# Chunk-wise loads and transposes, 256-token first blocks and an early exponential table in an attention and max-FFN kernel

## The chip, the cores and the metric

The kernel runs on one core of one Trainium2 chip. The metric is the time of one execution on the device in microseconds (us); lower is better. The kernel before took 203.25 us (median of 3 runs, 203.05 to 204.17).

Engines are named as in the profile: PE multiplies matrices, DVE and ACT do vector and scalar work, POOL does general work and issues most DMAs here, SP and ACT issue the rest. A DMA is a data transfer. "PEclk" in the profile is the granted PE clock as a share of full speed. Some executions fall in a slower state (of the changed kernel's four, two at 215.96 and 216.19 us against 211.87 and 213.48); each run is marked fast or slow, and comparisons here use fast runs alone. Spans read from a trace are about 1.8 us shorter than the run's time.

## The reference

```python
# q, k, v: (4, 8, 768, 64) = batch, head, token, dim;  n_sink = 4, window = 128
scores = q @ k.T / sqrt(64)
keep   = (key < n_sink) | (0 <= query - key < window)      # sink tokens and a sliding window
a      = softmax(where(keep, scores, -1e9))
x      = (a @ v) laid out as (3072 tokens, 512)
h      = max(x @ w1, x @ w2, x @ w3)                       # each (512, 768)
out    = h @ w_out                                         # (768, 512), float32
```

The kernel counts twelve chunks of 256 tokens, three to a batch of 768 tokens. Heads are handled in two groups of four.

## The kernel before

The kernel builds a list of tasks. Each has an engine, an assumed cost, what it depends on and a wished-for time. A planner (`arrange`) walks through assumed time and from that fixes the order of instructions on each engine. It does this while the kernel is built; on the chip the order stays. So an assumed number that is wrong changes an order, and in the traces below an instruction of DVE or POOL that waits holds up what stands behind it (DVE stands still for 13.60 us on one load).

```python
rate = 0.30                                    # assumed MB per us of one load

def load(name, mb, want, f, eng="POOL", cost=0.65, deps=()):
    t = task(eng, cost, f, deps=deps, want=want, name="i" + name)
    dma_done[name] = task("DMA", mb / rate, lambda: None, deps=[t], want=want, lat=2.0, name=name)
    return dma_done[name]

def sink_v(b, want):                           # the sink tokens' v, as a block-diagonal matrix
    def f():
        for g in range(NQ):                    # 2 groups x 4 heads x 2 = 16 copies of 0.5 KB per batch
            for i in range(4):
                for c in (1, 2):
                    j = 2 * g + c - 1
                    nc.sync.dma_start(
                        out=vbd[32 * j + 4 * i:32 * j + 4 * i + 4, b, j, 65 * i:65 * i + 65],
                        in_=vbufs[b % 2][0:n_sink, 4 * g + i, 0, :])
    ...
    t = task("SP", 1.6, f, deps=deps, want=want, name=f"vbd{b}")

# loads of batches 1 to 3: one row of 24 token rows per partition (the flat form)
nc.gpsimd.dma_start(out=raws[b, nm, g].rearrange("p j d -> p (j d)"),
                    in_=src[b, 4 * g:4 * g + 4].rearrange("i (p j) d -> (i p) (j d)", j=24))

BLOCKS = [[0], [1, 2], [3, 4], [5, 6], [7, 8], [9, 10], [11]]   # chunks of each FFN block
```

The line `vbd<-v_sb` in a profile is one of `sink_v`'s copies; `o<-vbd,e_sink` is the product that needs them (attention to the sink tokens, from chunk 1 on). `h<-xT,w_sb` are the FFN's first products, `y<-wo_sb,h_sb` its last, and `qT<-q_raw` a transpose on DVE.

The softmax here doesn't subtract the row's maximum and nothing guards it: scores larger than these inputs give would overflow.

## Time and profile before

| read from | before |
|---|---|
| median time | 203.25 us |
| span of the profiled run | 200.7 us |
| PE busy, up to 50 us (sum of five windows) | 30.8 of 50 us |
| DVE busy, 50 to 80 us | 29.3 of 30 us |
| FFN blocks begin (timeline of PE) | 18.9, 47.7, 79.2, 107.5, 135.4, 163.0, 185.6 us |

This is the first part of the page of the kernel before: its span, busy times, and then the span in 40 equal slices of 5 us, one digit a slice (busy tenths; 9 is 90% or more).

```profile
span 200.7 us, 4228 instructions
PE 172.7 (86%) x1680; PEld 95.7 (48%) x1680; DVE 135.7 (68%) x290; ACT 95.1 (47%) x146; POOL 36.7 (18%) x56
...
PE   0127997588979997999998999989999989999892
DVE  4358497587999999999917758636677276571450
...
PEclk9999999759999999999999999999999999999999
DMA  7999999999999910409920200140000410002202
```

Up to slice 10 (50 us) PE has holes while the DMA row is full: loads bind. From there DVE is full up to slice 20, and PE still has holes up to slice 16 (80 us): DVE binds. After that PE is full but for the last slices.

The next lines are from the timeline of the kernel before; columns are start in us, duration, engine, line, operation, output and inputs, shapes, count, and in brackets the idle time ahead of it and what ended it.

```profile
8.11 11.41 SPq L324 DMA_DIRECT2D vbd<-v_sb  x16
...
25.83 0.28 PE L412 MATMUL o<-vbd,e_sink 128*128 128x260 bf16 x1
26.89 0.82 POOL L237 DMA_DIRECT2D wo_sb<-in_moe_w_out_dram  x1 [0.45 <-DMA w_sb<-in_moe_w_dram]
28.33 0.56 POOL L258 DMA_DIRECT2D q_raw<-in_q_dram  x1 [0.62 <-DMA w_sb<-in_moe_w_dram]
...
42.71 3.76 PE L529 MATMUL y<-wo_sb,h_sb 128*128 128x512 bf16 x12
...
47.69 0.59 PE L510 MATMUL h<-xT,w_sb 128*128 128x512 bf16 x2
...
79.23 6.22 PE L510 MATMUL h<-xT,w_sb 128*128 128x512 bf16 x28
```

The sixteen sink copies of batch 0 occupy SP's sequencer for 11.4 us, from 8.1 us on; SP issues nothing else until 45.8 us, so they hold up no load there. POOL issues w_out's load at 26.9 us and goes straight on to chunk 3's q at 28.3 us. The attention product of chunk 1 runs at 25.8 us.

### The profile page before, as it was taken

Reading aid. Unit: us, or ns where it says so; the run is one execution under the profiler, and the core shown is the slowest. Engines: PE = TensorE matmul, PEld = TensorE weight load, DVE = VectorE, ACT = ScalarE, POOL = GpSimd, SP = SyncE. Lnnn points to the kernel's source line nnn. Section 1 sums busy time; section 2 is a strip of 40 time slices with the busy share of each in tenths; the row PEclk is TensorE's granted clock in tenths of the full one; section 3 lists DMA queues with packets and bytes.
Section 4 is the critical chain, followed back from the end, with each engine's and each line's share of the span. In section 5 each row is a group of like instructions: output and inputs, shape, how many; then the busy total and the mean of one; then the engine's idle time right before and its main releaser. Section 6 shows DMA issues by size and latency. Waiting matters only on the chain.

```text
span 200.7 us, 4228 instructions
## 1 busy us (share of the span) xinstructions
PE 172.7 (86%) x1680; PEld 95.7 (48%) x1680; DVE 135.7 (68%) x290; ACT 95.1 (47%) x146; POOL 36.7 (18%) x56
## 2 busy tenths in 40 slices
PE   0127997588979997999998999989999989999892
PEld 0023676433445544455554455554555544454770
DVE  4358497587999999999917758636677276571450
ACT  0344562634447548434668245665266592223422
POOL 7997648233200000022000000000000000000000
PEclk9999999759999999999999999999999999999999
DMA  7999999999999910409920200140000410002202
GB/s 125 207 160 154 197 172 198 213 180 172 255 173 177 195 63 1 156 4 80 82 106 1 105 4 0 42 170 0 3 0 5 157 52 3 0 0 106 108 0 104
DMA packets 41012, 19.72 MB, mean 98 GB/s; under 512 B 29472, under 2 KB 35872, under 8 KB 40992
## 3 DMA queue, kind: packets, MB, share of 16 engines
q0 software_dynamic: 36256, 12.07, 56.8%
q1 hardware_dynamic: 4352, 6.85, 9.6%
q10 hardware_dynamic: 384, 0.52, 1.0%
q8 instruction: 13, 0.21, 0.4%
q14 instruction: 7, 0.06, 0.1%
HBM read 25.17 MB, written 6.29 MB: 157 GB/s over the span
## 4 chain that ended last, share of the span: by engine, by line
PE 66%; DVE 21%; DMA 5%; issue 3%; ACT 3%; SPq 1%; DVEq 0%; ACTq 0%
PE h L510 39%; PE y L529 13%; PE st L390 6%; DMA q_f<-in_q_dram 5%; DVE kT L286 4%; DVE h_sb L521 4%; DVE x L434 4%; PE o L421 4%; DVE e_sb L403 4%; DVE qT L286 3%; PE xt L444 2%; ACT e_sb L395 2%; PE o L412 2%; DVE rc L431 1%; SPq L160 1%
## 5 line engine op out<-in xcount | busy, mean ns | idle before, releaser
L510 PE MATMUL h<-xT,w_sb 128*128 128x512 bf16 (+1 forms) x504 | 103.7, 353 | 1.8 <-ACT xT L451 1.2
L521 DVE TENSOR_TENSOR h_sb<-h,h_sb 128x512 bf16<-128x512 f32 (+1 forms) x84 | 51.4, 616 | 26.1 <-PE h L510 20.3
L510 PEld LDWEIGHTS <-w_sb 128*128 128x128 bf16 x504 | 46.8, 99 | 38.5 <-issue 2.6
L395 ACT ACTIVATE e_sb<-st 128x1024 bf16<-128x1024 f32 (+1 forms) x48 | 44.4, 953 | 14.4 <-PE st L390 14.4
L519 ACT CAST h_sb<-h 128x512 bf16<-128x512 f32 (+1 forms) x42 | 22.1, 526 | 47.6 <-PE h L510 47.3
L529 PE MATMUL y<-wo_sb,h_sb 128*128 128x512 bf16 x144 | 33.9, 387 | 0.1
L403 DVE TENSOR_TENSOR e_sb<-e_sb,mask 128x1024 bf16<-128x1024 bf16 (+1 forms) x48 | 29.7, 640 | 5.1 <-ACT e_sb L395 4.9
L390 PE MATMUL st<-qT,kT 32*128 32x128 bf16 (+1 forms) x512 | 15.9, 253 | 16.5 <-DVE kT L286 9.3
L536 ACT COPY y_sb<-y 128x512 f32<-128x512 f32 x24 | 14.1, 586 | 21.5 <-PE y L529 17.6
L390 PEld LDWEIGHTS <-kT 32*128 32x128 bf16 x512 | 10.9, 98 | 25.0 <-DVE kT L286 9.9
L434 DVE TENSOR_TENSOR x<-o,rc 128x256 bf16<-128x256 f32 x48 | 20.4, 424 | 1.7
L431 DVE RECIPROCAL rc<-o 128x4 f32<-128x4 f32 x48 | 8.5, 177 | 19.2 <-PE o L421 19.2
L529 PEld LDWEIGHTS <-h_sb 128*128 128x128 bf16 x144 | 13.8, 99 | 15.5 <-issue 1.6
L421 PEld LDWEIGHTS <-e_sb 128*128 128x128 bf16 x352 | 17.4, 102 | 6.5 <-DVE e_sb L403 1.5
L421 PE MATMUL o<-v_sb,e_sb 128*128 128x65 bf16 x352 | 19.4, 201 | 1.1 <-DVE h_sb L521 0.6
L451 ACT COPY xT<-xt 128x512 bf16<-128x512 bf16 x24 | 14.1, 588 | 9.2 <-PE xt L444 9.1
L444 PE MATMUL xt<-ident,x 128*128 128x128 bf16 x96 | 12.3, 230 | 5.1 <-DVE x L434 4.2
L265 POOL DMA_DIRECT2D v_sb<-in_v_dram x6 | 8.5, 1429 | 41.8 <-PE o L421 40.2
L286 DVE STREAM_TRANSPOSE kT<-k_raw 128x256 f32<-128x256 f32 x18 | 13.8, 826 | 0.0
L286 DVE STREAM_TRANSPOSE qT<-q_raw 128x256 f32<-128x256 f32 x18 | 13.7, 820 | 0.0
L444 PEld LDWEIGHTS <-x 128*128 128x128 bf16 x96 | 7.2, 99 | 12.5 <-DVE x L434 8.1
L412 PE MATMUL o<-vbd,e_sink 128*128 128x260 bf16 x32 | 9.2, 287 | 0.0
(35 smaller groups left out, 51.5 us busy)
## 6 DMA issues: line engine op xcount, KB each, us to landing
out_dram<-y_sb SPq DMA_DIRECT2D x24, 256.0 KB
w_sb<-in_moe_w_dram POOLq DMA_DIRECT2D x9, 256.0 KB, 8.4
q_raw<-in_q_dram POOLq DMA_DIRECT2D x6, 384.0 KB, 16.9
k_raw<-in_k_dram POOLq DMA_DIRECT2D x6, 384.0 KB, 16.6
v_sb<-in_v_dram POOLq DMA_DIRECT2D x6, 384.0 KB, 16.0
vbd<-v_sb SPq DMA_DIRECT2D x64, 0.5 KB
v_sb<-in_v_dram POOLq DMA_DIRECT2D x6, 128.0 KB, 7.7
wo_sb<-in_moe_w_out_dram POOLq DMA_DIRECT2D x1, 768.0 KB, 9.8
```

Source lines behind the costliest of these rows:

```text
L286: nc.vector.transpose(dst, src)
L390: nc.tensor.matmul(ps[:, i, col:col + n], lhsT=kT[r, key0:key0 + 128, e], rhs=qT[r, qq:qq + n, e], start=(e == 0), stop=(e == 1))
L395: nc.scalar.activation(st["e"][:, 2 * hh:2 * hh + 2, lo:], st["ps"][:, 2 * hh:2 * hh + 2, lo:], AF.Exp, scale=scale)
L403: nc.vector.tensor_tensor(out=ee, in0=ee, in1=m.unsqueeze(1).to_broadcast([128, 2, ncol]), op=ALU.mult)
L421: nc.tensor.matmul(o[:, i, :], lhsT=st["e"][:, i, col:col + 128], rhs=vbufs[b % 2][:, 4 * g + i, kb, :], start=(c == 0 and n == 0), stop=( ...
L434: nc.vector.tensor_tensor(out=st["x"][:, tt], in0=o[:, :, :D], in1=rc.unsqueeze(2).to_broadcast([128, 4, D]), op=ALU.mult)
L444: nc.tensor.transpose(st["xt"][:, n, 128 * tt:128 * tt + 128], x[:, 128 * n:128 * n + 128], ident)
L451: nc.scalar.copy(xTs[blk][:, 2 * g:2 * g + 2, off:off + 256], st["xt"])
L510: nc.tensor.matmul(ps[:, :ntok], lhsT=w_sb[:, wi, d, fb * 128:fb * 128 + 128], rhs=xTs[blk][:, d, :ntok], start=(d == 0), stop=(d == DSUB ...
L519: nc.scalar.copy(hs, ps[:, :ntok])
L521: nc.vector.tensor_tensor(out=hs, in0=ps[:, :ntok], in1=hs, op=ALU.max)
L529: nc.tensor.matmul(ps, lhsT=box["h"][:, fb, 128 * m:128 * m + 128], rhs=wo_sb[:, fb, :], start=(fb == 0), stop=(fb == FSUB - 1))
```

## The change

Its intent: load and transpose q and k of every batch by chunks of 256 tokens instead of by whole batches, so that a chunk can start earlier and transposes are cheaper; let the first FFN blocks have one chunk each; load less through SP and ACT at the start and load ACT's exponential table meanwhile. Beside this it moves the sink copies from SP to POOL, adds a product on POOL and two transposes on DVE that nothing uses, and raises the planner's `rate`. The core of the diff, cut, with some comments added:

```diff
-    rate = 0.30
+    rate = 0.40
...
-    for g in range(NQ):
-        load(f"q0{g}0", 0.26, g - 2000, qk_first("q", q, g), eng="SP", cost=0.4)
-        load(f"k0{g}0", 0.26, g - 2000, qk_first("k", k, g), eng="ACT", cost=0.4)
+    load("q0.0", 0.26, -2000, qk_first("q", q, 0), eng="SP", cost=2.7)
+    load("k0.0", 0.26, -2000, qk_first("k", k, 0), eng="ACT", cost=2.7)
...
+    task("ACT", 1.5, warm, deps=[t_one], want=-1999, name="warm")        # exponential table
+    def probe_pool():                                    # its result is used by nothing
+        nc.gpsimd.tensor_tensor(out=scratch.rearrange("p (a c) -> p a c", a=2),
+                                in0=scratch.rearrange("p (a c) -> p a c", a=2),
+                                in1=mask.unsqueeze(1).to_broadcast([128, 2, 512]), op=ALU.mult)
+    task("DVE", 1.2, probes, want=-999, name="probe")
+    task("POOL", 2.0, probe_pool, want=110, name="probe_pool")
...
+    def qk_chunk(nm, src, ch, g):                        # now for all twelve chunks
+        b, c = divmod(ch, NC)
+        def f():
+            s = src[b, 4 * g:4 * g + 4, 256 * c:256 * c + 256].rearrange("i (p j) d -> i p (j d)", j=8)
+            nc.gpsimd.dma_start(out=raw(nm, ch, g), in_=s)
...
-                        nc.sync.dma_start(
+                        nc.gpsimd.dma_start(
                             out=vbd[32 * j + 4 * i:32 * j + 4 * i + 4, b, j, 65 * i:65 * i + 65],
                             in_=vbufs[b % 2][0:n_sink, 4 * g + i, 0, :])
-        t = task("SP", 1.6, f, deps=deps, want=want, name=f"vbd{b}")
+        t = task("POOL", 9.0, f, deps=deps, want=nxt() if b == 0 else want, name=f"vbd{b}")
...
+            if ch >= NC:
+                qk_loads(ch, g)                          # q and k of a chunk, one head group
+                if c == 0 and g == 0:
+                    v_batch(b)                           # two loads, v of the whole batch
...
-BLOCKS = [[0], [1, 2], [3, 4], [5, 6], [7, 8], [9, 10], [11]]
+BLOCKS = [[0], [1], [2], [3, 4], [5, 6], [7, 8], [9, 10], [11]]
```

Cut are the rings and tiles, stores as tasks of their own, and a second way of transposing x that the constant `FIRST_BY_DMA = 99` turns off.

## The prediction

> **What bounds it now.** Span 200.7 us. By the windows view the kernel has three stages. Up to about 50 us PE is busy only 30.8 us: the page's DMA row stands at 9 tenths, and the timeline shows PE waiting for loads (FFN start at 18.9 us, chunk 2's transposes at 33.8, first output matmul at 42.7, slow after the idle time: 312 instead of 216 ns). From 50 to 80 us DVE binds (29.3 of 30 us busy; the chain of waits runs through transposes and max operations). From 80 us on PE binds: by the chain, 512-token blocks start at 79.3, 107.5, 135.5, 163.0 us, some 28 us each, and only about 6.6 us of PE idle time is left, most of it the tail. So the change can win mainly before 80 us.
>
> **What it removes or eases.**
> - The exponential table load (1.28 us) no longer delays the first k cast, and chunk 0's second head group (cast at 11.4 us) no longer waits for serial issues on SP and ACT.
> - Transposes: batches 1 to 3 used the 24-row form, 0.64 to 0.69 us apart in the timeline; the chunk form that batch 0 used stands 0.47 us apart. 36 x 0.19 = about 6 us less DVE work.
>
> **What it adds.** Two probe transposes at the start (estimate 1.3 us of DVE, while the first load runs); 72 more matmuls of half width and 12 more half-width max operations (24 x 0.36 against 12 x 0.62 us: +1.2 us DVE). The weights' pieces are unchanged.
>
> **What it moves, and why I expect little.** The bytes before w_out are the same, in nearly the same order[...]. So w_out still lands near 36.5 us (issued 26.9, landing 9.8 later). But the 16 tiny sink copies move from SP, where they ran from 8 to 19.5 us, to POOL behind w_out. POOL's DMAs wait for the one eight places back (order of instructions of the built kernel; in the trace POOL waits that way). The eighth sink copy therefore waits for w_out, the other nine cost about 0.55 us each: POOL is free for chunk 3 only near 42 us, and DMA runs dry meanwhile. The attention product of chunk 1, at 26 us before, now comes near 44 us. On DVE the transpose of chunk 3's q stands ahead of chunk 1's normalizations, so these wait for a load issued at 42 us, landed near 45. Hence PE is largely idle from about 31 to 44 us; block 1 starts near 49 us (before: 47.7, with more attention done). The lighter DVE then wins most of it back: the block of chunks 3 and 4 starts near 81 us (before 79.3), and later blocks run at 27.5 us.
>
> **Predicted:** 204.5 us, range 199 to 211; faster by over 2%: 0.15, within 2%: 0.55, slower: 0.30.
>
> **What would show it.** Right: the timeline has POOL issuing sink copies until about 42 us; DMA row dips near 38 to 43 us; first chunk-1 attention product after 40 us; DVE waits on chunk 3's q; transposes under 0.5 us apart. Wrong: chunk-1 product before 36 us, or block 1 starting before 46 us.
>
> **What would make it wrong.** Sink copies on POOL much cheaper (faster, near 198), or DVE and POOL disturbing each other so that issues stretch, or the slow PE state lasting longer after the idle time (slower, near 210).

## The result, and the profile after

The changed kernel took 214.72 us (median of 4 runs, 211.87 to 216.19; two of the four were slow). The ratio to the kernel before is 1.0454, with a 95% interval of 1.0368 to 1.0539: slower, outside the range predicted. Ratios here are the mean time of one kernel's fast runs over that of the other's fast runs of the same rounds, so they are not quite the ratio of the medians quoted. The fast run with the profile took 213.48 us, the other fast one 211.87 us; the median of 214.72 us lies above both because of the two slow runs.

The same part of the page, of the changed kernel:

```profile
span 211.7 us, 4423 instructions
PE 175.8 (83%) x1752; PEld 104.5 (49%) x1752; DVE 136.1 (64%) x304; ACT 94.3 (45%) x152; POOL 90.3 (43%) x147
...
PE   0047983754959999999959999999999999999892
DVE  6358657004668899999999377992638827552360
...
PEclk9999999587979999999996999999999999999999
DMA  5999999149999918995179920005000040002202
```

POOL's busy time has gone from 36.7 to 90.3 us. DVE's row has two zeros (slices of 5.3 us here, so 37 to 48 us), the DMA row falls to 1 and 4 in the same two, and the clock row has 5, 8, 7 around the stretches where PE idled. The twelve output products behind the 4.05 us wait took 5.15 us, 429 ns each, and the granted clock from 38.6 to 43.8 us was 0.53; in c_rate below the same twelve took 229 ns each at a clock of 1.00. In the kernel before, the clock stood at 0.50 from 37.9 to 43.0 us behind a wait of PE of only 1.95 us (PE was busy 0.88 of the 2.9 us from 35.0 us on), so its twelve (the line at 42.71 us above, 313 ns each, clock 0.73) were slowed as well. What lowers the clock, and after how long a wait, is not shown.

The timeline of the changed kernel, lines of POOL, DVE and PE:

```profile
29.43 0.83 POOL L257 DMA_DIRECT2D wo_sb<-in_moe_w_out_dram  x1 [0.97 <-DMA w_sb<-in_moe_w_dram]
30.62 0.55 POOL L344 DMA_DIRECT2D vbd<-v_sb  x1 [0.36 <-issue]
...
38.85 4.45 POOL L344 DMA_DIRECT2D vbd<-v_sb  x9 [2.79 <-DMA wo_sb<-in_moe_w_out_dram]
43.29 0.73 POOL L180 DMA_DIRECT2D q_raw<-in_q_dram  x1
44.02 0.69 POOL L180 DMA_DIRECT2D k_raw<-in_k_dram  x1
44.71 2.88 POOL L296 DMA_DIRECT2D v_sb<-in_v_dram  x2
47.58 0.72 POOL L180 DMA_DIRECT2D q_raw<-in_q_dram  x1
...
49.60 0.64 DVE L308 STREAM_TRANSPOSE qT<-q_raw 128x256 f32<-128x256 f32 x1 [13.60 <-DMA q_raw<-in_q_dram]
...
38.62 5.15 PE L578 MATMUL y<-wo_sb,h_sb 128*128 128x512 bf16 x12 [4.05 <-DMA wo_sb<-in_moe_w_out_dram]
43.60 0.28 PE L435 MATMUL o<-vbd,e_sink 128*128 128x260 bf16 x1
...
54.01 1.63 PE L559 MATMUL h<-xT,w_sb 128*128 128x256 bf16 x12
...
88.80 5.34 PE L559 MATMUL h<-xT,w_sb 128*128 128x512 bf16 x24
```

Read it as a chain. w_out is issued at 29.4 us. The sink copies stand behind it in POOL's order; the last nine go out only when w_out, issued eight places ahead of the first of them, has landed (38.6 us); whether this belongs to the chip or to the way the kernel is built was not tested. POOL then needs 4.45 us for nine copies, about half a microsecond each, and comes to chunk 3's q at 43.3 us, against 28.3 us before. Of the 12.7 us from the first copy to that q, POOL is busy issuing copies for 8.0 us and waits for 4.6 us, 2.79 us of it for w_out. That q lands at 49.6 us. The DVE was waiting for it from 36.0 us on, with chunk 1's normalizations behind it in its order; their attention products came at 43.6 us. Hence block 1 begins at 54.0 us, and the block of chunks 3 and 4 at 88.8 us, against 79.2.

There is a second place. These are the lines of the changed kernel's timeline around 107 us:

```profile
106.12 0.55 DVE L426 TENSOR_TENSOR e_sb<-e_sb,mask 128x768 bf16<-128x768 bf16 x1
...
107.14 3.44 DVE L426 TENSOR_TENSOR e_sb<-e_sb,mask 128x768 bf16<-128x768 bf16 x1
...
108.03 2.13 POOL L280 TENSOR_TENSOR scratch<-scratch,mask 128x1024 bf16<-128x1024 bf16 x1
...
110.64 0.23 PE L444 MATMUL o<-v_sb,e_sb 128*128 128x65 bf16 x2 [2.46 <-DVE e_sb L426]
...
111.64 7.03 PE L578 MATMUL y<-wo_sb,h_sb 128*128 128x512 bf16 x24
```

The same masking product takes 0.55 us, and 3.44 us when POOL's unused product runs beside it. PE waits 2.46 us for it. After the wait the granted clock is 0.50 from 112 to 115 us, so the 24 output products that follow are slow too (7.03 us).

The spans differ by 11.0 us (211.7 less 200.7). The starts of FFN blocks divide this up:

| stretch | before | after | difference |
|---|---|---|---|
| up to the block of chunks 3 and 4 | 79.2 | 88.8 | +9.6 |
| that block to the next | 28.2 | 30.9 | +2.7 |
| from there to the last block's start | 78.1 | 76.5 | -1.6 |
| last block to the end | 15.1 | 15.4 | +0.3 |

### The profile page after: what moved, and what is told of

Read it like the earlier page. It is cut to its first block, busy times and chain, and to the rows that moved or that the text cites. A ratio compares the mean times of both kernels' runs of the same rounds, so it can differ in the third digit from the quotient of the medians.

```text
span 211.7 us, 4423 instructions
## 1 busy us (share of the span) xinstructions
PE 175.8 (83%) x1752; PEld 104.5 (49%) x1752; DVE 136.1 (64%) x304; ACT 94.3 (45%) x152; POOL 90.3 (43%) x147
## 4 chain that ended last, share of the span: by engine, by line
PE 65%; DMA 18%; POOL 9%; DVE 3%; issue 2%; ACT 2%; ACTq 0%; POOLq 0%
PE h L559 39%; PE y L578 14%; DMA q_raw<-in_q_dram 9%; PE st L413 4%; DMA w_sb<-in_moe_w_dram 4%; DMA wo_sb<-in_moe_w_out_dram 4%; PE o L444 4%; POOL vbd L344 2%; PE xt L473 2%; DVE e_sb L426 2%; PE o L435 1%; POOL q_raw L180 1%; POOL w_sb L191 1%; POOL v_sb L296 1%; ACT e_sb L418 1%
## 5 line engine op out<-in xcount | busy, mean ns | idle before, releaser
L559 PE MATMUL h<-xT,w_sb 128*128 128x256 bf16 (+1 forms) x576 | 106.2, 332 | 4.1 <-DVE h_sb L570 2.3
L559 PEld LDWEIGHTS <-w_sb 128*128 128x128 bf16 x576 | 53.9, 100 | 37.8 <-issue 4.2
L570 DVE TENSOR_TENSOR h_sb<-h,h_sb 128x256 bf16<-128x256 f32 (+1 forms) x96 | 53.1, 555 | 26.3 <-PE h L559 18.4
L568 ACT CAST h_sb<-h 128x256 bf16<-128x256 f32 (+1 forms) x48 | 23.2, 483 | 47.2 <-PE h L559 47.2
L578 PE MATMUL y<-wo_sb,h_sb 128*128 128x512 bf16 x144 | 36.5, 413 | 4.0 <-DMA wo_sb<-in_moe_w_out_dram 4.0
L344 POOL DMA_DIRECT2D vbd<-v_sb x64 | 32.0, 507 | 18.1 <-DMA v_sb<-in_v_dram 6.7
L426 DVE TENSOR_TENSOR e_sb<-e_sb,mask 128x1024 bf16<-128x1024 bf16 (+1 forms) x48 | 32.9, 699 | 4.8 <-ACT e_sb L418 4.7
L308 DVE STREAM_TRANSPOSE qT<-q_raw 128x256 f32<-128x256 f32 x24 | 15.1, 635 | 21.3 <-DMA q_raw<-in_q_dram 21.3
L180 POOL DMA_DIRECT2D k_raw<-in_k_dram x23 | 15.7, 683 | 11.8 <-DMA q_raw<-in_q_dram 4.0
L473 PE MATMUL xt<-ident,x 128*128 128x128 bf16 x96 | 12.7, 234 | 6.8 <-DVE x L463 6.8
L308 DVE STREAM_TRANSPOSE kT<-k_raw 128x256 f32<-128x256 f32 x24 | 15.1, 628 | 4.0 <-PE st L413 2.4
L180 POOL DMA_DIRECT2D q_raw<-in_q_dram x23 | 16.0, 694 | 3.6 <-DVE rc L454 1.9
```

The lines of the kernel that those rows point to most:

```text
L180: nc.gpsimd.dma_start(out=raw(nm, ch, g), in_=s)
L308: nc.vector.transpose(dst, src)
L344: nc.gpsimd.dma_start(out=vbd[32 * j + 4 * i:32 * j + 4 * i + 4, b, j, 65 * i:65 * i + 65], in_=vbufs[b % 2][0:n_sink, 4 * g + i, 0, :])
L426: nc.vector.tensor_tensor(out=ee, in0=ee, in1=m.unsqueeze(1).to_broadcast([128, 2, ncol]), op=ALU.mult)
L473: nc.tensor.transpose(st["xt"][:, n, 128 * tt:128 * tt + 128], x[:, 128 * n:128 * n + 128], ident)
L559: nc.tensor.matmul(ps[:, :ntok], lhsT=w_sb[:, wi, d, fb * 128:fb * 128 + 128], rhs=xTs[blk][:, d, :ntok], start=(d == 0), stop=(d == DSUB ...
```

## The experiments

All twelve kernels gave correct results. Three theories stood at the start.

- A: the sink copies in POOL's queue are the main cause, because they hold back the loads that follow.
- P: POOL's unused product costs the stretch around 107 us.
- K: loads of the chunk form land later than the flat ones (I had counted some 3 us), and that is what starves DVE. This is a rival of A for the stretch before 80 us; a further rival is the split into 256-token blocks.

The first expectations call A "Theory S" and its rival, here K, "Rival L"; where an expectation names a theory otherwise, it says what it holds. Later the planner's `rate` came in as a fourth cause. Block starts in us, read from each timeline, with times. The medians are over all runs of a kernel; those of "after" (two of four) and a_no_probe (one of four) hold slow runs, so compare these two by their ratios. Block 1 has 512 tokens in before, b_sink_pool, c_blocks_before and b_first_chunk, and 256 in the others.

| kernel | block 1 | chunks 3 and 4 | next block | median time | ratio to before (95%) |
|---|---|---|---|---|---|
| before | 47.7 | 79.2 | 107.5 | 203.25 | 1 |
| after | 54.0 | 88.8 | 119.7 | 214.72 | 1.0454 (1.0368 to 1.0539) |
| a_sink_sp_same | 47.7 | 78.9 | 105.5 | 200.07 | 0.9857 (0.9788 to 0.9926) |
| a_no_probe | 53.8 | 89.1 | 115.7 | 209.85 | 1.0310 (1.0249 to 1.0371) |
| a_sink_sp_noprobe | 41.6 | 77.8 | 104.4 | 197.62 | 0.9710 (0.9661 to 0.9759) |
| b_sink_pool | 53.9 | 95.7 | 124.2 | 218.21 | 1.0727 (1.0647 to 1.0806) |
| c_blocks_before | 48.3 | 79.9 | 106.6 | 199.54 | 0.9829 (0.9772 to 0.9886) |
| a_rate | 48.9 | 86.5 | 114.1 | 206.54 | 1.0139 (1.0083 to 1.0196) |
| c_rate | 33.6 | 72.5 | 99.1 | 192.33 | 0.9467 (0.9426 to 0.9508) |
| b_first_chunk | 46.3 | 77.8 | 106.0 | 200.99 | 0.9872 (0.9830 to 0.9914) |

### The sink copies on SP again: a_sink_sp_same

One word of the changed kernel; the order of all other instructions stays.

```diff
-                        nc.gpsimd.dma_start(
+                        nc.sync.dma_start(
                             out=vbd[32 * j + 4 * i:32 * j + 4 * i + 4, b, j, 65 * i:65 * i + 65],
```

> The changed kernel with the 64 sink copies issued by SP instead of POOL; the order of the instructions on every other engine is kept. Theory S (the copies in POOL's queue hold up chunk 3's loads, and DVE waits for them): chunk 3's first q load is issued near 31 us instead of 43.3, lands near 40, the 13.6 us DVE wait shrinks below 5 us, FFN block 1 starts near 46 us instead of 54, and the time falls by 6 to 9 us, to about 206. Rival L (the chunk-wise loads themselves are too slow, whatever stands before them): the time falls by less than 3 us.

It took 200.07 us (four runs, 198.9 to 201.19). By the ratios that is 6.0% of the time before, 12.1 us, less than the changed kernel: more than I had expected. Its timeline:

```profile
10.09 12.38 SPq L344 DMA_DIRECT2D vbd<-v_sb  x16
...
29.98 0.73 POOL L180 DMA_DIRECT2D q_raw<-in_q_dram  x1 [0.21 <-issue]
...
40.68 0.64 DVE L308 STREAM_TRANSPOSE qT<-q_raw 128x256 f32<-128x256 f32 x1 [4.94 <-DMA q_raw<-in_q_dram]
...
78.92 5.34 PE L559 MATMUL h<-xT,w_sb 128*128 128x512 bf16 x24
```

POOL reaches chunk 3's q at 30.0 instead of 43.3 us, DVE waits 4.94 instead of 13.60 us, and the block of chunks 3 and 4 begins at 78.9 instead of 88.8 us. So 9.9 us of the loss up to that block are the copies' place in POOL's queue: theory A is shown, since nothing else was moved. How much of this is the wait for w_out in POOL's queue and how much the issue time of the copies was not separated. The 26.6 us to the next block (30.9 in the changed kernel) come on top: POOL's product came at 84.0 us here and stretched no DVE instruction.

### Without POOL's unused product: a_no_probe

```diff
-    task("POOL", 2.0, probe_pool, want=110, name="probe_pool")
+    task("POOL", 2.0, lambda: None, want=110, name="probe_pool")
```

> The changed kernel without the useless POOL product, all else in the same order. Theory P (the mask multiplication that took 3.44 us instead of 0.55 at 107 us was blocked by POOL's product): no mask multiplication above 0.75 us, PE's wait of 2.5 us at 108 us is gone, time 2 to 3 us lower (about 212). Rival (the long multiplication has another cause): it is still there, time unchanged.

It took 209.85 us, and its ratio is 1.4% of the time before, 2.9 us, below that of the changed kernel. The two intervals just touch, so the reading rests on the traces. The same two masking products in its timeline:

```profile
106.37 0.55 DVE L426 TENSOR_TENSOR e_sb<-e_sb,mask 128x768 bf16<-128x768 bf16 x1
107.39 0.55 DVE L426 TENSOR_TENSOR e_sb<-e_sb,mask 128x768 bf16<-128x768 bf16 x1
```

Both take 0.55 us, and that stretch of the kernel takes 26.6 instead of 30.9 us: 4.3 us back in the trace. Of these, 2.46 us are PE's wait, and about 1.7 us the slow clock after it: here the clock is 1.00 from 112 to 115 us, and the output products take 5.34 us (23 of the 24 are in the trace) instead of 7.03. Theory P is shown for this place. How POOL's product stretches DVE's is not shown. DVE's product is stretched only beside POOL's, and ends 0.4 us after it (110.58 and 110.16 us). But 3.44 us is 0.76 us more than the two together (0.55 and 2.13), and by the trace DVE's product began 0.89 us before POOL's and, at 0.55 us, would have been over by then; spans on POOL are rough, and which of the two came first is not shown. It is not a fixed charge, either. In a_rate below POOL's product came at 67.6 us, beside a transpose (0.65 us as elsewhere) and normalizations; the one masking product that began in its last 0.2 us took 0.65 instead of 0.55 us.

### Both, with the tasks arranged anew: a_sink_sp_noprobe

```diff
-    task("POOL", 2.0, probe_pool, want=110, name="probe_pool")
+    task("POOL", 2.0, lambda: None, want=110, name="probe_pool")
...
-                        nc.gpsimd.dma_start(
+                        nc.sync.dma_start(
...
-        t = task("POOL", 9.0, f, deps=deps, want=nxt() if b == 0 else want, name=f"vbd{b}")
+        t = task("SP", 10.0, f, deps=deps, want=want, name=f"vbd{b}")
```

> The same move, but with the instruction order arranged anew for it, and without the useless POOL product. Theory S: the attention product of chunk 1 comes back to about 27 us, FFN block 1 can fill PE before w_out lands, the 512-token block of chunks 3 and 4 starts near 75 us or earlier (changed kernel: 88.8), and the time is near 200 us or below. Rival L: still above 208 us, with DVE waiting for q chunks.

It took 197.62 us, 2.9% less than the kernel before. The time is as expected; the block of chunks 3 and 4 came at 77.8 us, later than the 75 us expected. So the rest of the change is a gain, which two of its parts had hidden. DVE still waits 4.10 us at 49 us for the second head group's q of chunk 3.

### The move made in the kernel before: b_sink_pool

```diff
-                        nc.sync.dma_start(
+                        nc.gpsimd.dma_start(
...
-        t = task("SP", 1.6, f, deps=deps, want=want, name=f"vbd{b}")
+        t = task("POOL", 9.0, f, deps=deps, want=nxt() if b == 0 else want, name=f"vbd{b}")
```

> The kernel before with only the sink copies moved to POOL behind w_out, as in the change. Theory S: the loads of batch 1 are issued some 10 us later, FFN block 1 starts some 7 us later than 47.7 us, time 208 to 212. Rival L: the position of the copies does not matter, time within 2 us of before.

It took 218.21 us, 7.3% more than the kernel before and well above what I had expected. These lines show its waits of PE (in all, times, longest) and, from the timelines, a POOL and a PE line:

```profile
PE o L412 <- DMA vbd<-v_sb: 16.6, 3, 8.2
```

```profile
38.18 1.97 POOL L324 DMA_DIRECT2D vbd<-v_sb  x4 [2.88 <-DMA wo_sb<-in_moe_w_out_dram]
...
83.57 0.37 PE L412 MATMUL o<-vbd,e_sink 128*128 128x260 bf16 x1 [8.19 <-DMA vbd<-v_sb]
```

The first stall is the one of the changed kernel. The second, which I had not foreseen, is at 83.6 us: the copies of batch 1 stand in POOL's order behind the loads of batch 3, and those wait for buffers; then the copies themselves wait for these loads and others, one by one, from 67.9 to 82.6 us. So theory A holds in both kernels, and its size depends on what the copies stand behind.

### What a chunk load costs by itself: b_load_shapes

Eight more loads into an unused tile in the kernel before, at a time with no other load; output stores ran beside some of them. Each waits for the one ahead of it.

```diff
...
+        by_head = q[0, 0:4, 0:256].rearrange("i (p j) d -> i p (j d)", j=8)
+        flat = q[0].rearrange("h (p j) d -> (h p) (j d)", j=8)[0:128]
+        for n in range(4):
+            nc.gpsimd.dma_start(out=probe, in_=by_head)
+            nc.gpsimd.dma_start(out=probe, in_=flat)
```

> The kernel before, with eight extra loads of 128x512 f32 to bf16 appended to POOL's queue, when no other load runs, one after the other into one scratch tile, each waiting for the landing of the one before: in turn the form of a chunk load (4 heads x 32 rows in DRAM) and a flat one (128 rows in DRAM), of the same bytes and the same 1024-byte writes. Theory K[...]: a chunk form lands 5 to 6.5 us after its issue, a flat one 2.5 to 3.5 us, about 2.3 us apart or more. Rival (a small load has a long latency whatever its form; the 6.3 us came from the queue behind it): both the same within 0.5 us. The time of the kernel itself should stay that of before, as POOL is idle then.

The run took 204.41 us (one look; the eight loads are extra work). Its source views of the two lines, chunk form first and then flat form, end with the time from issue to landing:

```profile
DMA to landing us min/median/max: 5.3/5.8/6.5
```

```profile
DMA to landing us min/median/max: 3.0/3.1/3.2
```

The same 128 x 512 values land after 5.8 us in the chunk form and after 3.1 us in the flat one (medians). The pair with no other load or store beside it landed after 5.3 and 3.0 us. The 3.1 us fit what I had put into the prediction; the changed kernel's loads are of the other form. The packets differ too: the chunk form has 528, 128 with data and 400 of 4 bytes; the flat one has 144, 16 of them of 4 bytes (from the pages: b_first_chunk, with two chunk loads more through POOL, has 1056 packets more in queue q0 than the kernel before, and this run with its eight loads 2688 more). Whether the small packets make the loads slow was not tested.

So theory K is right about the size of a load, but it did not cause the loss by itself: with the same loads and the copies on SP, the kernel took 200.07 us. It goes into A's size: q was issued at 43.3 us and landed 6.3 us later, and the second group's q, issued at 47.58 us behind v's two loads, took 11.7 us.

### The blocks of before: c_blocks_before

From a_sink_sp_noprobe, with the first three chunks in two blocks.

```diff
-BLOCKS = [[0], [1], [2], [3, 4], [5, 6], [7, 8], [9, 10], [11]]
+BLOCKS = [[0], [1, 2], [3, 4], [5, 6], [7, 8], [9, 10], [11]]
```

> The version with the sinks on SP and no POOL product, but with the blocks of before (256, then 512 tokens). If the short first blocks give the early stage its gain, as intended: slower by 3 to 5 us than that version (200.5 to 202.5). Rival (they only add half-width work; the gain comes from the lighter DVE): same or faster, 196 to 198.

It took 199.54 us, 1.9 us more than its base by the medians and less than I had expected. So the 256-token blocks are no cause of the loss; in that version they are worth about 2 us.

### The table alone: b_exp_early

In the kernel before, a tiny exponential at the start of ACT's tasks:

```diff
...
+    t_one = task("DVE", 0.1, lambda: nc.vector.memset(warm_sb, 0.0), want=-1001, name="one")
+    task("ACT", 1.5, warm, deps=[t_one], want=-1998.5, name="warm")
```

> The kernel before with only the exponential table loaded early. The first scores can start 1.3 us earlier, but the second head group is cast only at 11.4 us and the weights land later, so I expect no gain: within 0.7 us of before. Rival (it lies on the critical path): 1 us or more faster.

It took 203.02 us, ratio 0.9988 (0.9938 to 1.0037). But this experiment failed as a test: ACT issues eight DMAs first, so the table came at 6.42 us where it had been at 6.21. It was not early.

### The start of the change alone: b_first_chunk

So this part was done again in the kernel before, with what makes room for the table: chunk 0's second head group is loaded through POOL.

```diff
-    for g in range(NQ):
-        load(f"q0{g}0", 0.26, g - 2000, qk_first("q", q, g), eng="SP", cost=0.4)
-        load(f"k0{g}0", 0.26, g - 2000, qk_first("k", k, g), eng="ACT", cost=0.4)
+    load("q000", 0.26, -2000, qk_first("q", q, 0), eng="SP", cost=2.7)
+    load("k000", 0.26, -2000, qk_first("k", k, 0), eng="ACT", cost=2.7)
+    load("q010", 0.26, -2000, qk_chunk("q", q, 1, 0))
+    load("k010", 0.26, -2000, qk_chunk("k", k, 1, 0))
...
+    task("ACT", 1.5, warm, deps=[t_one], want=-1999, name="warm")
```

> The kernel before with only the start of the change: chunk 0's second head group of q and k loaded in bf16 through POOL, four loads less on SP and ACT, and the exponential table loaded while the first k load is under way (in the earlier run with the table alone it was still issued behind all eight k loads, at 6.4 us, so that run did not test an early table). Theory: the start gains nothing. The second group's loads land at 7.5 to 9 us, the k cast runs near 7.2 us, but the scores cannot start before about 10 to 11 us because DVE transposes the second group first; the first FFN block starts at 18.5 to 21 us, and from there on the stage up to 50 us is bound by the order of loads, which stays: 202.5 to 205 us, same. Rival (the intent of the change: an earlier start is worth something): first FFN block before 17.5 us and below 201.5 us.

The table was at 2.69 us now, and the kernel took 200.99 us, ratio 0.9872 (0.9830 to 0.9914): 1.3% faster. I had expected no gain, and the rival had expected an FFN start before 17.5 us; neither is right. The first FFN block began at 23.0 us, later than the 18.9 us of before, and yet block 1 began 1.4 us earlier. The windows view, first of the kernel before and then of this one, has for 30 to 40 us the busy times of PE, PEld, DVE, ACT and POOL, the granted clock, the DMA share and GB/s:

```profile
30.00:40.00 10.00, 6.66 (x114) 5.19 (x111) 6.24 (x16) 4.32 (x7) 6.03 (x8) 0.90 1.32 205
```

```profile
30.00:40.00 10.00, 7.66 (x134) 6.02 (x131) 7.94 (x22) 6.15 (x10) 6.39 (x8) 1.00 1.39 180
```

PE did more work there and kept its full clock; it fell later (0.83 from 40 to 50 us, where it was 0.76 before). Between 33 and 39 us PE has one wait of 1.69 us here, and waits of 0.89, 0.49 and 1.95 us before; whether this kept the clock up was not tested. All starts from block 1 on stay 1.4 us earlier, and the order of the early DVE work changed as well.

### The planner's rate: a_rate, c_rate, c_rate_only, c_v_last_rate

The change also raised the rate the planner assumes. a_rate puts this one number back in the changed kernel, with the copies left on POOL:

```diff
-    rate = 0.40
+    rate = 0.30
```

> The changed kernel with one number of its planner put back: the assumed transfer rate of loads, 0.30 instead of 0.40 (before had 0.30). Sink copies stay in POOL's queue, the POOL product stays. The planner now puts the transpose of chunk 3's q behind chunk 1's normalizations and the first max operations of block 1. Theory A (the loss before 80 us needs both: POOL held by sink copies until about 43 us, and DVE standing on chunk 3's q): the chunk-1 attention product still comes at about 43.6 us, but block 1 starts near 47 instead of 54.0 us, the block of chunks 3 and 4 near 84 to 86 instead of 88.8, time 207 to 211 us against 214.7. Rival (only POOL being held matters, the place of the transpose does not): 213 to 215 us, the block of chunks 3 and 4 at 88 or later.

It took 206.54 us, a little under the range expected, but not for all of the reason given. Here the transpose of chunk 3's q stands behind chunk 1's normalizations. Block 1 began at 48.9 instead of 54.0 us, but the block of chunks 3 and 4 at 86.5 (expected 84 to 86): 2.3 us were won up to there. With that transpose out of the way PE waits for the sink copies themselves, 12.4 us in four waits, this one the longest:

```profile
40.38 0.38 PE L435 MATMUL o<-vbd,e_sink 128*128 128x260 bf16 x1 [6.72 <-DMA vbd<-v_sb]
```

Another 3.2 us were won because POOL's product fell at 67.6 us, where it stretched no masking product by more than 0.1 us; the next stretch took 27.7 instead of 30.9 us. So while POOL is held by the copies, the place of that transpose matters little at chunks 3 and 4.

c_rate is a_sink_sp_noprobe with the rate at 0.30 and the assumed latency of a load at 4.0 instead of 2.0 us:

```diff
-    rate = 0.40
+    rate = 0.30
...
-        dma_done[name] = task("DMA", mb / rate, lambda: None, deps=[t], want=want, lat=2.0, name=name)
+        dma_done[name] = task("DMA", mb / rate, lambda: None, deps=[t], want=want, lat=4.0, name=name)
```

> The version with the sinks on SP and no POOL product, but the build-time arrangement told that loads are slower (0.30 instead of 0.40 MB per us, 4 instead of 2 us of latency), so that DVE's transposes stand later in its order and block 1's FFN stands ahead of w_out's first use. If in-order waiting of DVE for late q chunks is what is left of the early loss (2.2 us at 31 and 4.1 us at 49 us in that version): those waits shrink below 1 us each, the block of chunks 3 and 4 starts near 74 us instead of 77.8, time 194 to 196 us. Rival (DMA's throughput sets the early stage): the start stays within 1 us, time about 197.5.

It took 192.33 us (191.94 to 192.59), 5.3% less than the kernel before and, with c_rate_only, the best of all; I had expected 194 to 196 us. Lines of its page, and the waits of DVE for q in the changed kernel and in this one (in all, times, longest):

```profile
PE   0016999999997799999999999999999999999992
...
PEclk9999999999999999999999999999999999999999
```

```profile
DVE qT L308 <- DMA q_raw<-in_q_dram: 21.3, 5, 13.6
```

```profile
DVE qT L308 <- DMA q_raw<-in_q_dram: 3.5, 1, 3.5
```

Here DVE waits once for a q, at the start. The planner now starts block 1's first products before block 0's output products (at 33.6 us), so PE has work while w_out is under way, and no slice of its clock row falls below 9.

c_rate_only has only the rate put back, with the latency left at 2.0:

> The version with the sink copies on SP and without the POOL product, with the rate alone put back to 0.30 and the latency left at 2.0 us (the earlier version also raised it to 4.0 and took 192.3 us). The order of the early DVE work is the same as there. If the rate alone does it: 192 to 193 us; if the latency was needed: 194 to 198 us.

It took 192.33 us, the same. So the rate alone does it. c_v_last_rate is c_rate with the two large v loads of a batch behind its first four q and k loads:

```diff
-                if c == 0 and g == 0:
+                if c == 0 and g == NQ - 1:
                     v_batch(b)
```

> The version of 192.3 us (sink copies on SP, no POOL product, rate 0.30, latency 4.0) with the two large v loads of a batch issued after its first four q and k loads instead of between them. Theory K (the second head group's q of chunk 3 waits behind v's 1.57 MB): in the version with rate 0.40 this wait cost 4.1 us of DVE; at rate 0.30 the planner already puts the transpose late enough that DVE waits for it 0 us, so here little is left to gain: 191 to 193 us. Rival (the large loads in between still hold up the next batches): below 190 us.

It took 192.7 us: nothing is left to gain there once DVE hardly waits for a q (3.9 us in all).

## Why the prediction was wrong, point by point

- **What bounded the kernel: right.** Loads bind before 50 us, DVE to 80 us, PE after that. The difference arose ahead of the block of chunks 3 and 4, but for POOL's product.
- **Sink copies on POOL: the mechanism was right.** Predicted were copies until about 42 us (measured 43.3), chunk 1's attention product near 44 (43.6), DVE waiting on chunk 3's q (13.6 us), a dip of the DMA row, transposes 0.48 us apart (31.34 and 31.82 us in the timeline). One figure was misread: for the same 128 x 256 values the 24-row form is 0.60 to 0.64 us apart in the trace of the kernel before, not 0.64 to 0.69, so the saving in transposes was nearer 5 us (an estimate: 36 x 0.14) than the 6 us predicted. One copy takes 0.50 us to issue and 2.4 us (median) from issue to landing. It is their number that counts: 64 copies of 0.5 KB occupied POOL for 32.0 us, and moving them alone took 9.9 us off the start of the fourth block.
- **The step that failed: "these wait for a load issued at 42 us, landed near 45".** It was issued at 43.3 us and landed at 49.6. I had counted 3 us, which is what a quiet flat load takes (3.1 us); the chunk form takes 5.3 us even when nothing else runs, and took 6.3 us here. From this, block 1 came at 54.0 us and not "near 49" (a_rate, with that transpose moved behind the normalizations, has it at 48.9). Chunks 3 and 4 came at 88.8 and not "near 81", which is 7.8 us of the miss; of these the wait explains a part (a_rate wins back 2.3 us there), and how the rest divides was not tested. Two more terms sat in it: the second group's q took 11.7 us, and w_out landed at 38.6 instead of the 36.5 us which I had kept, because it was issued 2.5 us later.
- **A term that was missing: POOL's product.** I had counted it as useless but free. It cost 4.3 us in the trace, by stretching one DVE instruction and by the slow clock of PE behind the wait.
- **"The lighter DVE then wins most of it back": too hopeful in its place.** The stretch after chunks 3 and 4 became 1.6 us shorter (26.6 us without POOL's product, 28.2 before) and the rest up to the last block another 1.6 us. I put these down to the lighter DVE; no run isolates it, and its busy time fell by only 2.6 us (135.7 to 133.1 in a_no_probe). In the changed kernel it gave nothing before 80 us, where DVE stood waiting for loads instead of working.
- **The sum.** Predicted were 204.5 us, or 202.7 of span; measured 211.7, 9.0 more. Chunks 3 and 4 account for 7.8 of these. From there on POOL's product and the later gains come to 1.2 us more than I had counted.
- **The start.** I counted its gain into a stage where loads bind, and so near zero. Alone it is worth 2.6 us by b_first_chunk's medians. I had missed the cost of `rate` altogether: it decided where a transpose stood in DVE's order. It is worth little in the changed kernel up to chunks 3 and 4, but 5.3 us by the medians once the copies are off POOL (197.62 to 192.33).

That leaves open why chunk loads land later than flat ones (5.8 against 3.1 us), how the loss before chunks 3 and 4 divides between the wait for w_out, the issue time of the copies and slow landings, and why b_first_chunk gains exactly what it does.

## What to carry to other kernels

Before you move small DMAs to another issuing engine, ask what stands behind them in that engine's order: here sixteen issues of half a microsecond, and the waits among them, put the first load of chunk 3 at 43.3 instead of 30.0 us (a_sink_sp_same). Take the landing time of a load from a load of the same access pattern, not from one of the same size (here 5.8 and 3.1 us for the same values); and in a kernel ordered by a planner, treat an assumed rate as part of the program, for here one number was worth 5 us. An instruction whose result nobody uses can still cost (here 4.3 us), if it runs beside the wrong instruction of the engine that matters.
